# The expert loop's tiles in another sequence, a fourth raw buffer, and second products that take all high parts first

## Chip, cores and metric

One core of a Trainium2 chip. The metric is the device time of one execution in microseconds (us), and lower is better. TensorE's clock has two levels, 1.2 and 2.4 GHz, and the profile gives the granted level as a share of the higher one.

## What is computed

Three parts follow each other. The first is attention over 4 x 8 heads of 576 positions (one attention on means of four positions, one in a narrow window). The second is a mixture of experts, and the change touches only this one. The third is a token and channel mixing network. The reference of the second part, cut to what matters:

```python
for s in range(S):
    e = fresh_e if s == 0 or local_gate[b, s] < 0.5 else prev_e
    h = np.maximum(x[b, s] @ w1[e], 0.0)      # 512 -> 1024
    out[b, s] = p[e] * (h @ w2[e])            # 1024 -> 512
```

## The kernel before

**Number format.** Every float32 operand of the expert products is split into a high and a low part (both of a type that TensorE multiplies at its full rate), and a product is made of three matmuls: high times high, high times low, low times high (`three`, L1125). So each weight block costs a cast on ACT (`wh`) and a subtraction on DVE (`wl`), and each hidden block costs a ReLU on ACT (`hh`) and one operation on DVE (`hl`, `relu`, L1132).

**The expert loop** (`Moe.run`, L1477) goes over eight ranks of experts, most tokens first, with room for 384, 376, 320, 288, 256, 256, 192 and 128 tokens (`CAPS`), and for each over eight blocks of 128 hidden columns. A block loads 512 KB of raw weights into a `raw` tile (`fetch`, L1196, on SP's queue), splits them (`loadw`, L1205), makes the first product into a PSUM tile `m` (`mm1`, L1236), and one block later the second product into one to three PSUM tiles `y` of 128 tokens each (`mm2`, L1269). There are two `m` and four `y` tiles. After an expert's last block the `y` tiles are copied to `yo` and stored to `yd`. The tokens of an expert are fetched by indirect transfers from POOL into `xg` (`gather`, L1215), 128 at a time, transposed by TensorE and split into `xh` and `xl`. Five `xg` tiles exist, three `raw` tiles, and a ring of four `wh` and four `wl` (one of each, `l_wh` and `l_wl`, is filled before the loop). For the last expert (128 tokens) the first product reads `raw` and `xg` directly. In between, 21 jobs convert the weights of the mixing stage (`convert`, L1141: `cr`, `cf`, `cs`, on DVE, ACT and POOL), and a memset on POOL and ten stores on SP zero the unused rows of `yd` (`zeros`, L1464).

**The order of the work** comes from a planner in the kernel (`Sched.order`, L406). It keeps for every engine the time at which it is free, takes the operation that can start first (ties within 0.02 go to the longer remaining path less a stage time), and hands each operation a free tile of its pool. The engines then execute the lists in order. All matmuls of an `mm2` are one operation for it. It plans each stage by itself, from time 0. For the expert loop TensorE counts as free from 2.0 (`PE_LATE`) and all others from 0.

**Where tiles lie.** A tile lies behind the one allocated before it. The loop's tiles take over bytes of attention's tiles, and the first writer of a tile waits for the last users of the bytes below. In bytes of a partition, attention's tiles are: pt0 and pt1 141760 to 154048, kd 154048 to 158656, vd 158656 to 166848, od and ptd to 176064, p0 and p1 176064 to 180160, pc0 180160 to 182208, pc1 to 184256, xn to 188352, small ones above. p and pc hold results of two experts that are computed early, and are stored to `yd` by transfers from ACT's queue; pc's are the last work before the loop. The loop's tiles of before are: cr, cf, cs, yo and h 105376 to 137120, zero to 139168, raw0 to raw2 139232 to 151520, wh0 to wh2 to 163808, wl0 to wl2 to 176096, xg0 176096 to 178144, xg1 to 180192, xg2 to 182240, xg3 to 184288, xg4 to 186336, xh0 and xl0 to 198624.

Of the kernel before, what the change touches and what calls it, by code (L numbers as in the profile page):

```python
# [4 lines left out]
F32 = mybir.dt.float32  # L5
F32R = mybir.dt.float32r
BF16 = mybir.dt.bfloat16
F16 = mybir.dt.float16
I32 = mybir.dt.int32
# [8 lines left out]
DM = H * D  # L18
# [6 lines left out]
CAPS = [384, 376, 320, 288, 256, 256, 192, 128]  # L25
# [10 lines left out]
KF = FF // 128  # L36
# [1138 lines left out]
class Experts:  # L1175
# [11 lines left out]
    after = first = ready = ()  # L1187
# [78 lines left out]
    def hidden(self, C):  # L1266
        return self.new("hh")[:, 0:C], self.new("hl")[:, 0:C], None

    def mm2(self, r, fb, h):  # L1269
        S_ = self.S  # L1270
        hh, hl, both = h
        C = self.caps[r]
        T = -(-C // 128)
        wh, wl = (w[:, DM:2 * DM] for w in self.w[KF * r + fb][0:2])
        m = 0 if both is None else self.part(C)
        if fb == 0:
            self.y = [self.new("y") for _ in range(T)]
        for k in range(T):
            if k % self.CUT == 0:
                g = S_.group("pe", after=self.after)  # L1280
                g.__enter__()
            n = min(128, C - 128 * k)
            c = slice(128 * k, 128 * k + n)
            if n == m:
                two = [(2 * n, both, wh), (n, hh[:, c], wl)]
                for rows, x, w in two if fb == 0 else two[::-1]:
                    S_.i("pe", "matmul", out=self.y[k][0:rows], lhsT=x, rhs=w, start=(fb == 0 and rows > n), stop=(fb == KF - 1 and rows > n))
            else:
                three(S_, self.y[k][0:n], (hh[:, c], hl[:, m + c.start:m + c.stop]), (wh, wl), fb == 0, fb == KF - 1)
            if (k + 1) % self.CUT == 0 or k == T - 1:  # L1290
                g.__exit__(None, None, None)
        if self.ready:
            self.after = self.first + (len(S_.ops) - 1,)
        if fb == KF - 1:
            for k in range(T):
                n = min(128, C - 128 * k)
                t = self.result(r, k)
                if n == m:
                    self.i("act", "copy", out=t[0:n], in_=self.y[k][n:2 * n])
                    self.i("dve", "tensor_tensor", out=t[0:n], in0=t[0:n], in1=self.y[k][0:n], op=ALU.add)  # L1300
                elif k % 2 == 0:
                    self.i("act", "copy", out=t[0:n], in_=self.y[k][0:n])
                else:
                    self.i("dve", "tensor_copy", out=t[0:n], in_=self.y[k][0:n])
                r0 = self.rows[r] + 128 * k
                self.i(self.QUEUE, "dma_start", out=self.yd[r0:r0 + n, :], in_=t[0:n])
# [115 lines left out]
class Moe(Experts):  # L1422
    LO, CUT, QUEUE = "dve", 4, "dma"

    def __init__(self, ctx, tc, at, rt, xd, yd, wx, jobs, lead):
        self.rt, self.xd, self.jobs = rt, xd, jobs
        S_ = Sched(tc)
        pool = lambda n, b, **kw: ctx.enter_context(tc.tile_pool(name=n, bufs=b, reuse_waits="tile", **kw))
        sa, sp, pt, pp = pool("ma", 1), pool("ms", 1), pool("mt", 1, space=PSUM), pool("mp", 1, space=PSUM)
        self.sp = sa  # L1430
        for name, shape, dt, n in (
            ("cr", [128, 1024], I32, 2), ("cf", [128, 512], I32, 2), ("cs", [128, 512], F32, 2),
            ("yo", [128, DM], F32, 3), ("h", [128, 2 * CAPS[0]], F32R, 3),
            ("raw", [128, 1024], F32, RAW), ("wh", [128, 1024], F32R, RING - NLEAD), ("wl", [128, 1024], F32R, RING - NLEAD),
            ("xg", [128, DM], F32, 5), ("xh", [128, 4, CAPS[0]], F32R, 1), ("xl", [128, 4, CAPS[0]], F32R, 1),
        ):
            p = sp if name in ("raw", "wh", "wl", "xg", "xh", "xl") else sa
            S_.pool(name, [p.tile(shape, dt, name=f"{name}{j}") for j in range(n)])
        for name, n in (("t", 2), ("m", 2), ("y", 4)):
            S_.pool(name, [(pt if name == "t" else pp).tile([128, 512], F32, name=f"{name}{j}") for j in range(n)])  # L1440
        super().__init__(S_, tc, at, yd, wx, CAPS, ROW0, lambda r: rt.eri[0:1, r:r + 1],
                         lambda r, k, n: rt.xi[0:n, r, k:k + 1], xd[:, :])
        self.ident = at.ident
        self.held = {n: [S_.held(n, t) for t in ts] for n, ts in lead.tiles.items()}
        self.x[0] = tuple(self.held[n][0] for n in ("xh", "xl"))
        for n in range(NLEAD):
            self.w[n] = self.held["wh"][n], self.held["wl"][n], None
# [29 lines left out]
    def run(self):  # L1477
        NW = KF * NE
        prev, done = None, []
        t0 = 0.0  # L1480
        for n in range(NW):
            r, fb = divmod(n, KF)
            self.S.stage = t0
            t0 += 4 * (12 * CAPS[r] / 2400 + TILES[r] * 0.65)
            if n >= NLEAD:
                self.loadw(n)
            if fb == 3 and r + 1 < NE:
                self.gather(r + 1)
            h = self.mm1(r, fb)
            if prev is not None:  # L1490
                self.mm2(*prev)
            prev = (r, fb, h)
            done.append(len(self.S.ops) - 1)
            if n == 24:
                self.S.stage = t0
                self.zeros()
            if n >= 8 and n % CONV == 0 and self.jobs:
                self.S.stage = t0 + 60
                convert(self.S, *self.jobs.pop(0), after=(done[n - 6],))
        self.mm2(*prev)  # L1500
        assert not self.jobs
        self.S.issue(self.S.order(busy=dict(pe=PE_LATE)))
        at, cold = self.at, self.S.pools["t"][1][0][:, 264:512]
        for _ in range(TAIL):
            self.nc.tensor.matmul(cold, at.onesb, at.rb, start=True, stop=True)
# [270 lines left out]
KDVE = ((0, 0), (0, 1), (1, 0), (1, 1), (2, 0), (2, 1), (3, 0), (3, 1))  # L1776
STEP, D_LEAD, R_LAG = 14.0, 2.0, 0.5
SLACK = 0.02
PE_LATE = 2.0
NLEAD, CONV, C2_EARLY = 1, 2, 4  # L1780
RAW, RING = 3, 4
RING_F, TOK_FB = 26, 3
MIX_WARM = 10.0, 0.5
MARK = 1, 0
SHIFT = {('d1', 0): -6, ('load_q', 0): -11, ('x1', 3): 14, ('load_u', 0): 1, ('route', 2): -8, ('load_u', 3): -14, ('d1', 1): 14, ('route', 3): 18, ('x1', 0): 5, ('l1', 3): 2, ('l1', 0): -5, ('d2', 2): -1, ('Lead', 'gather'): -8, ('Early', 'gather'): -22, ('l2', 3): 2, ('pool_k', 1): -2, ('l2', 1): 1, ('pool_v', 3): -4, ('route', 1): 3, ('Early', 'mm2'): 2, ('pool_q', 0): -4, ('d1', 3): 3, ('pool_q', 2): -10, ('pool_k', 0): -5, ('load_q', 3): 1, ('pool_q', 3): -1, ('load_u', 1): 1, ('load_u', 2): 7, ('l2', 2): -2, ('d2', 0): -5, ('load_q', 2): 3}
WARM0 = 0.0
# [23 lines left out]
```

## Time and profile before

| | us |
|---|---|
| median of 3 runs | 817.35 |
| lowest and highest | 811.60 and 822.07 |
| the profiled execution, its time | 818.32 |
| the profiled execution, its span | 816.5 |
| mean granted TensorE clock | 0.982 |

The span has three stages: attention up to about 205 us, the expert loop up to 441.9 us, and after a hand-over of some ten the mixing stage to the end. The profile is of one execution. Its rows give, for every instruction, its engine, the line of the kernel, the tiles that it writes and reads, its start and duration, and in brackets the idle time before it with what ended that. All loop instructions are issued from lines L548 to L552, so the tiles' names tell them apart: `m` is a first product, `y` a second one, `t` a transpose. An arrow `<-` reads "made from" between tiles and "released by" before an engine.

### The profile page before, as it was taken

What the parts mean: (1) busy time and instruction counts of PE and PEld (TensorE: products, weight loads), DVE (VectorE), ACT (ScalarE), POOL (GpSimd) and SP (SyncE); (2) the same over time, 40 slices, a digit from 0 to 9 for tenths busy, and PEclk for the clock granted to TensorE, in tenths of its full rate; (3) what the DMA queues carried; (4) which work ended last, traced back from release to release, by engine and by line L of the source; (5) the groups of instructions that cost most, each with busy time, mean ns of one, the idle gap of its engine ahead of it and who ended that gap; (6) DMA issues with size and microseconds to landing.
All of it is one profiled execution on the core that took longest, in us unless ns stands there. A gap on an engine that the chain in (4) does not pass through costs nothing. (4 is left out here: it accounts for less than half of the span.)

```text
span 816.5 us, 14043 instructions
## 1 busy us (share of the span) xinstructions
PE 768.3 (94%) x5377; PEld 645.6 (79%) x5377; DVE 468.9 (57%) x1064; ACT 331.3 (41%) x722; POOL 195.9 (24%) x158
## 2 busy tenths in 40 slices
PE   7878898999899998999898999999999999999998
PEld 5666775898787977887796787888888888888897
DVE  6789898698366878889952667532441244121121
ACT  1767886554344554666552535320321032111110
POOL 3325313111423545525400155200000000000000
PEclk9999999999899999999999999999999999999999
DMA  9988344556588775867653224002000200010010
GB/s 267 223 224 225 98 130 129 165 176 238 187 295 287 248 255 170 279 224 253 205 196 133 82 91 123 26 26 71 14 1 26 71 14 1 0 52 1 1 52 27
DMA packets 36348, 107.92 MB, mean 132 GB/s; under 512 B 5003, under 2 KB 5643, under 8 KB 35895
## 3 DMA queue, kind: packets, MB, share of 16 engines
q1 hardware_dynamic: 32359, 95.15, 37.1%
q0 software_dynamic: 3200, 10.28, 4.2%
q10 hardware_dynamic: 720, 1.57, 0.5%
q8 instruction: 43, 0.70, 0.4%
q14 instruction: 26, 0.21, 0.1%
HBM read 87.32 MB, written 19.66 MB: 131 GB/s over the span
## 5 line engine op out<-in xcount | busy, mean ns | idle before, releaser
L552 DVE SCALAR_TENSOR_TENSOR x_h<-x_m,x_h 128x512 fp32r<-128x512 f32 (+1 forms) x60 | 38.2, 637 | 194.9 <-ACT x_h L552 192.5
L548 PE MATMUL x_y<-x_h,c2h 128*128 128x512 f32 (+1 forms) x480 | 136.2, 369 | 0.0
L552 ACT ACTIVATE x_h<-x_m 128x512 fp32r<-128x512 f32 (+1 forms) x60 | 33.3, 555 | 201.0 <-PE x_m L548 176.0
L548 PEld LDWEIGHTS x_y<-x_h,c2h 128*128 128x128 f32 x480 | 86.6, 189 | 14.4
L548 PE MATMUL x_y<-x_h,c2l 128*128 128x512 f32 (+1 forms) x240 | 88.3, 368 | 0.0
L548 PE MATMUL y<-wh,h 128*128 128x512 f32 (+2 forms) x205 | 75.9, 408 | 4.2 <-DVE h L552 2.8
L552 DVE TENSOR_TENSOR wl<-raw,wh 128x1024 fp32r<-128x1024 f32 (+1 forms) x47 | 60.4, 1287 | 19.7 <-ACT wh L552 19.2
L552 ACT CAST wh<-raw 128x1024 fp32r<-128x1024 f32 (+1 forms) x47 | 46.9, 1001 | 25.6 <-PE y L548 15.5
L552 POOL TENSOR_SCALAR cs<-cs 128x512 f32<-128x512 f32 (+1 forms) x21 | 38.0, 1810 | 57.6 <-ACT cs L552 57.2
L548 PEld LDWEIGHTS x_y<-x_h,c2l 128*128 128x128 f32 x240 | 45.2, 189 | 7.6
L548 PEld LDWEIGHTS y<-wh,h 128*128 128x128 f32 (+2 forms) x205 | 38.7, 190 | 15.4 <-DVE h L552 5.0
L548 PE MATMUL y<-wl,h 128*128 128x512 f32 (+3 forms) x112 | 44.7, 399 | 0.0
L552 POOL TENSOR_TENSOR cf<-cf,cs 128x512 f32<-128x512 f32 (+1 forms) x21 | 37.7, 1797 | 28.2 <-DVE cf L552 26.4
L552 DVE SCALAR_TENSOR_TENSOR h<-m,h 128x256 fp32r<-128x256 f32 (+3 forms) x88 | 29.4, 356 | 10.1 <-ACT h L552 9.9
L1169 POOL DMA_INDIRECT xg<-xd,q_xi x19 | 19.4, 1020 | 56.2 <-PE t L550 19.5
L552 ACT ACTIVATE h<-m 128x256 fp32r<-128x256 f32 (+6 forms) x64 | 25.4, 397 | 17.7 <-PE m L548 14.6
L552 DVE SCALAR_TENSOR_TENSOR cf<-cr,cf 128x512 int32<-128x512 int32 (+1 forms) x42 | 30.4, 725 | 0.7
L548 PE MATMUL m<-l_xh,wh 128*128 128x256 f32 (+2 forms) x96 | 29.2, 304 | 1.0 <-DVE h L552 1.0
L548 PE MATMUL y<-l_wh,h 128*128 128x512 f32 (+2 forms) x75 | 28.8, 424 | 1.3 <-DVE h L552 1.1
L548 PE MATMUL pv<-pt,vw 128*64 128x96 f32 x384 | 22.5, 263 | 7.6 <-ACT pt L552 4.6
L548 PE MATMUL m<-l_xh,wl 128*128 128x256 f32 (+2 forms) x96 | 28.8, 300 | 0.0
L548 PE MATMUL m<-l_xl,wh 128*128 128x256 f32 (+2 forms) x96 | 28.8, 300 | 0.0
(813 smaller groups left out, 2022.0 us busy)
## 6 DMA issues: line engine op xcount, KB each, us to landing
raw<-in_wx SPq DMA_DIRECT2D x80, 512.0 KB
cr<-in_c SPq DMA_DIRECT2D x16, 512.0 KB
vw<-in_vw SPq DMA_DIRECT2D x12, 512.0 KB
kz<-in_kw SPq DMA_DIRECT2D x24, 200.0 KB
xd<-xn SPq DMA_DIRECT2D x16, 256.0 KB
yd<-zero SPq DMA_DIRECT2D x8, 512.0 KB
yd<-yo SPq DMA_DIRECT2D x15, 256.0 KB
x_cr<-in_c SPq DMA_DIRECT2D x7, 512.0 KB
```

What stands on the lines that cost most here:

```text
L548: f(kw.pop("out"), **kw)
L552: f(**kw)
L1169: nc.gpsimd.indirect_dma_start(out=t.real()[0:n, :], out_offset=None, in_=table, in_offset=bass.IndirectOffsetOnAxis(ap=index, axis=0))
```

## The change

The tiles of the loop are allocated in the sequence of two lists of names (`PLACE`). The first list has the same sequence as before. The second one puts the xg tiles behind the raw tiles, and ends with wl1. There are four raw tiles. The planner counts TensorE as free from 8.0, ACT from 6.5 and DVE from 7.5. In `mm2` of the loop (not of the two experts computed early, whose `CUT` is 1) a new function `halves` issues, for all tiles, high times high and high times low, and after them low times high for all tiles. The number of matmuls stays.

By the sizes of the tiles the second list gives: raw0 to raw3 139232 to 155616, xg0 to xg4 155616 to 165856, xh0 to 172000, wh0 to 176096, wh1 to 180192, wh2 to 184288, wl2 to 188384, wl0 to 192480, xl0 to 198624, wl1 to 202720.

```diff
+    def halves(self, fb, h, ys, wh, wl, m):
+        hh, hl, both = h
+        mm = lambda y, x, w, start, stop: self.S.i("pe", "matmul", out=y, lhsT=x, rhs=w, start=start, stop=stop)
+        first, last = fb == 0, fb == KF - 1
+        o = 0
+        two = []
+        for k, y in enumerate(ys):
+            n = y.a.shape[0]
+            c = slice(o, o + n)
+            o += n
+            if n != m:
+                mm(y, hh[:, c], wh, first, False)
+                mm(y, hh[:, c], wl, False, False)
+                two.append((y, hl[:, m + c.start:m + c.stop], wh, False, last))
+            else:
+                tall = self.y[k][0:2 * n]
+                if first:
+                    two += [(tall, both, wh, True, False), (y, hh[:, c], wl, False, False)]
+                else:
+                    mm(y, hh[:, c], wl, False, False)
+                    two.append((tall, both, wh, False, last))
+        for x in two:
+            mm(*x)
...
-        for k in range(T):
+        if self.CUT >= T:
+            with S_.group("pe", after=self.after):
+                self.halves(fb, h, [self.y[k][0:min(128, C - 128 * k)] for k in range(T)], wh, wl, m)
+        for k in range(T) if self.CUT < T else ():
...
-        self.S.issue(self.S.order(busy=dict(pe=PE_LATE)))
+        self.S.issue(self.S.order(busy=LATE))
...
-PE_LATE = 2.0
+LATE = dict(pe=8.0, act=6.5, dve=7.5)
...
-RAW, RING = 3, 4
+RAW, RING = 4, 4
...
+PLACE = ("cr0 cr1 cf0 cf1 cs0 cs1 yo0 yo1 yo2 h0 h1 h2",
+         "raw0 raw1 raw2 raw3 xg0 xg1 xg2 xg3 xg4 xh0 wh0 wh1 wh2 wl2 wl0 xl0 wl1")
```

## Rows read from the trace of the kernel before

**Rows 1.** The page's first part: busy us, share of the span, instructions of each engine.

```profile
PE 768.3 (94%) x5377; PEld 645.6 (79%) x5377; DVE 468.9 (57%) x1064; ACT 331.3 (41%) x722; POOL 195.9 (24%) x158
```

**Rows 2.** Table by stretches: length, busy us by engine, clock, transfer share, GB/s.

```profile
204.85:217.66 12.81, 8.95 (x39) 7.68 (x37) 4.71 (x6) 4.35 (x7) 7.24 (x8) 0.73 0.44 138
217.66:322.80 105.14, 99.42 (x524) 86.79 (x522) 74.46 (x110) 51.19 (x81) 45.95 (x29) 1.00 0.77 256
322.80:327.65 4.85, 4.83 (x18) 4.10 (x19) 3.17 (x6) 3.08 (x6) 1.11 (x1) 0.65 0.64 188
...
340.00:400.00 60.00, 55.63 (x343) 47.31 (x342) 55.64 (x76) 36.40 (x59) 29.47 (x17) 1.00 0.71 234
...
424.30:434.70 10.40, 8.64 (x58) 7.39 (x56) 4.03 (x9) 4.10 (x11) 0.00 (x0) 1.00 0.72 225
434.70:440.40 5.70, 5.68 (x31) 5.15 (x31) 1.97 (x4) 2.13 (x5) 0.00 (x0) 0.70 0.29 119
```

**Rows 3.** List of TensorE's waits, 204 to 442: us in total, times, longest.

```profile
PE y L548 <- DVE h L552: 3.9, 6, 1.0
PE t L550 <- DMA xg<-xd,q_xi: 3.9, 1, 3.9
PE m L548 <- DVE h L552: 2.9, 3, 1.5
PE m L548 <- DMA raw<-in_wx: 1.8, 1, 1.8
PE m L548 <- DVE wl L552: 1.8, 1, 1.8
PE y L548 <- DVE yo L552: 1.3, 3, 0.6
```

**Rows 4.** The loop's start, by engine: start, duration, engine, operation, idle before.

```profile
205.08 0.34 PE L548 MATMUL m<-l_xh,l_wh 128*128 128x384 f32 x1
207.18 0.60 PE L550 MATMUL t<-ident,xg 128*128 128x128 f32 x4
...
217.69 0.42 PE L548 MATMUL m<-l_xh,wh 128*128 128x384 f32 x1
...
208.19 0.94 POOL L1169 DMA_INDIRECT xg<-xd,q_xi  x1 [16.41 <-DMA yd<-pc]
...
194.95 1.45 SPq L1200 DMA_DIRECT2D raw<-in_wx  x3
...
205.31 0.93 ACTq L552 DMA_DIRECT2D yd<-pc  x2
207.37 0.49 ACT L552 ACTIVATE h<-m 128x384 fp32r<-128x384 f32 x1 [1.50 <-PE m L548]
...
212.76 0.59 ACT L552 CAST xh<-t 128x512 fp32r<-128x512 f32 x1 [4.36 <-PE t L550]
213.24 1.99 ACT L552 CAST wh<-raw 128x1024 fp32r<-128x1024 f32 x2
...
214.32 2.36 DVE L552 TENSOR_TENSOR wl<-raw,wh 128x1024 fp32r<-128x1024 f32 x2 [0.25 <-issue]
```

**Rows 5.** List of waits of SP's queue, 204 to 442.

```profile
SPq L552 <- POOL zero L546: 20.5, 1, 20.5
```

**Rows 6.** In order of time: TensorE's four transposes and the next product.

```profile
329.93 0.60 PE L550 MATMUL t<-ident,xg 128*128 128x128 f32 x4
330.29 0.38 PE L548 MATMUL m<-xh,l_wh 128*128 128x288 f32 x1
```

**Rows 7.** In order of time: a second product's wait for DVE's h.

```profile
379.06 0.40 PE L548 MATMUL y<-wh,h 128*128 128x512 f32 x1
379.30 0.39 PE L548 MATMUL y<-wl,h 128*128 128x512 f32 x1
380.65 0.73 PE L548 MATMUL y<-wh,h 128*128 128x512 f32 x2 [0.96 <-DVE h L552]
```

More of the change, by code (lines that the diff above doesn't have):

```diff
@@ L1430, in __init__ @@
         self.sp = sa
[L1431 to L1438, printed above, removed]
+        shapes = dict(cr=([128, 1024], I32), cf=([128, 512], I32), cs=([128, 512], F32), yo=([128, DM], F32),
+                      h=([128, 2 * CAPS[0]], F32R), raw=([128, 1024], F32), wh=([128, 1024], F32R), wl=([128, 1024], F32R),
+                      xg=([128, DM], F32), xh=([128, 4, CAPS[0]], F32R), xl=([128, 4, CAPS[0]], F32R))
+        tiles = {}
+        for p, names in ((sa, PLACE[0]), (sp, PLACE[1])):
+            for x in names.split():
+                name, j = x.rstrip("0123456789"), x[len(x.rstrip("0123456789")):]
+                tiles.setdefault(name, {})[int(j)] = p.tile(*shapes[name], name=x)
+        for name, ts in tiles.items():
+            S_.pool(name, [ts[j] for j in sorted(ts)])
         for name, n in (("t", 2), ("m", 2), ("y", 4)):
```

## The prediction

> **What bounds the kernel now.** I read the page first, for the shares: TensorE is busy for 94% of the span and no other engine for more than 57% [rows 1]. So only time that TensorE lacks can be gained, and the question is where it lacks any. The change touches one stage, the expert loop, which runs from about 205 to 441.9 us. I took the table by stretches next [rows 2], then the list of TensorE's waits inside that loop [rows 3]. In it the reader sees eight kinds of wait, and the six largest add up to 3.9 + 3.9 + 2.9 + 1.8 + 1.8 + 1.3 = 15.6 us. To these come three stretches at a granted clock below 1: 0.73, 0.65 and 0.70 [rows 2]. Each of them begins with one of the long waits (3.9, 1.8 and 1.8 us). In the last two the lower of the two levels (1.2 instead of 2.4 GHz) costs 4.85 x 0.35 = 1.7 us and 5.7 x 0.30 = 1.7 us on top of the wait. The mixing stage behind the loop is TensorE alone and none of its instructions change.
>
> Then I read the loop's first 13 us in order of time [rows 4]. TensorE does the first product of block 0 from 205.08 to 207.18, a group of four transposes, and stops. The transposes of the next rows wait for a gather that POOL could only issue at 208.19, released by the transfer yd<-pc. The ACT queue then shows the consequence: the cast xh at 212.76 comes after 4.36 us of idle time, and the cast of block 1's weights, wh, stands behind it at 213.24, although the raw weights were asked for at 194.95. Block 1's first product starts at 217.69.
>
> Why a gather waits for a transfer out of pc can be seen in the addresses. The gather's target xg1 covers bytes 178144 to 180192, and pc0 begins at 180160: they share 32 bytes. xg2 and xg3 lie on pc0 and pc1 wholly.
>
> The same transfer also stops SP. The memset of the zero tile is in POOL's queue behind those gathers, and SP waited 20.5 us for it [rows 5]. Every later raw load is behind that in SP's queue.
>
> **The change, part by part.** The sum is made against the profiled execution: 818.32 us, of which 816.5 are the span and 1.8 lie around it. That is 0.97 above the median of the runs shown.
>
> *Sequence of tiles and the planner's start times, taken together.* After the change the five xg tiles lie at 155616 to 165856, on kd and vd, which attention has left long before. So POOL can issue five gathers without the wait for yd<-pc, the memset follows them, and SP is no longer held. The planner now believes that TensorE comes free at 8.0, ACT at 6.5 and DVE at 7.5 instead of at 2, 0 and 0. With raw weights landing before that, I expect its list to put the casts of blocks 1 to 3 first on ACT, then h of block 0, and on TensorE block 0's first product, block 1's first product, block 0's second product. The transposes then move to where their stage time puts them, about block 3.
>
> What the old start costs: from 205.08 to 217.69 are 12.6 us. The work in it at full clock is 2.1 for the product (twelve, to 207.18), four groups of transposes at 0.36 (329.93 to 330.29 [rows 6]), so 1.4, and nine products of 512 columns at 0.23 to 0.24 (379.06 to 379.30 [rows 7]), so 2.1: 5.6 us. The excess is 7.0 us.
>
> What the new start costs: ACT is done with its last transfer of attention at 205.31 + 0.93 = 206.24. A cast takes 1.0 and DVE's wl 1.18 [rows 4], so wl of block 1 is there at 208.4. The first two products of block 1 need only wh; the third stops TensorE from about 207.2 to 208.4: 1.2 us. The wait for pc doesn't vanish either. It moves to the weights: wh1 now covers 176096 to 180192, again 32 bytes of pc0, and wh2 lies on pc0 and pc1. ACT's second cast so starts at about 208.2, the third ends at 210.2, and h of block 0 (0.49) behind them at 210.7, against block 1's first product ending at 208.4 + 10 x 0.17 = 210.1 (2.1 over twelve is 0.17): 0.6 us. Queued behind those casts on ACT are h and, through h, DVE's lower half. Sum: 7.0 - 1.8 = 5.2 us gained. Bounds: 7.0 if the list hides both stalls, and 1.5 if the new gap of 1.2 grows to the 1.8 that let the clock fall elsewhere (0.6 + 1.7) and the casts cost another 1.4 behind pc. I take 5.2, because every term of it has a row.
>
> *High parts first.* No product is added or removed, and no weight load. What moves is the place of the first product that needs DVE's half of h. TensorE waited 3.9 us in six places for it [rows 3], all between 369 and 402 us, where blocks have 256 columns and two tiles. One of the six is shown [rows 7]: two products at 379.06 and 379.30, then 0.96 us idle. The old order already put two products ahead of the wait; the new one puts four. So the cover grows by 2 x 0.23 = 0.46 us, not by the whole wait. Six waits so give 6 x 0.46 = 2.8 us at most. DVE is busy for 55.64 of the 60 us there [rows 2], so a part of what is gained will be late again at the next subtraction for wl. Ends: 0 and 2.8; I take 2.0.
>
> The same move has a price at the seven changes of expert. There the second and third tile's accumulators are asked for 0.23 and 0.46 us sooner, while yo still empties them. Three such waits are in the list, 1.3 us together [rows 3]. Ends: 0 and 3 x 0.46 = 1.4; I take +0.7.
>
> *Fourth raw buffer.* It adds no transfer. Its cover is for the last expert, whose blocks of 128 columns are so short that weights come late: one wait of 1.8 us [rows 3], then 1.7 us through the clock [rows 2], 3.5 in all. A fourth load in flight can remove both if the transfer engines have room. They moved 225 GB/s at a share of 0.72 there, against 256 GB/s at 0.77 as a mean over the loop's first 105 us [rows 2], so there is some room. Ends: 0 and 3.5; I take 2.5. The Trainium skill ("Trainium Kernel Development and Optimization", Key Constraints) speaks against it: transfers from SP, ACT and POOL all run on the same 16 engines, so another load in flight makes none faster. If those engines were the limit in the tail, this term would be 0 and the time 809.8; the row of 0.72 says that they aren't.
>
> *The middle.* The list is planned anew from other start times, so the remaining waits (m for DVE's h 2.9, wl 1.8 with 1.7 of clock [rows 2, 3]) will fall elsewhere. They come from DVE being late against its plan, which the change doesn't mend. A load that is there sooner lets ACT's casts go sooner, and DVE has 30.7 us to spare from 217.66 to 322.80 [rows 2]. Ends: -6.4, all gone, and +3.5, one more stall like the one at 322.8 (wait and clock). I take -1.0.
>
> Sum: -5.2 - 2.0 + 0.7 - 2.5 - 1.0 = -10.0 us. 818.32 - 10.0 = 808.3, and 0.97 lower against the median: 807.35. I predict 807.
>
> **The rivals.** *Everything goes.* The start gives 7.0, high parts 2.8, the tail 3.5 and the middle half or all of its 6.4: together 16.5 to 19.7, so 797 to 801. For it speaks DVE's spare time early in the loop; against it 93% busy DVE at 340 to 400.
>
> *Little of it stays.* Either the waits are kept per pool and not by bytes, so that the gather goes on waiting and only other terms gain, or what the terms behind the start win is lost again at DVE in 340 to 400. Then 1.5 to 5.2 remain, and the time is 812 to 816. Against the first: the loop's first three raw loads were issued at 194.95, ten us before pc's transfer [rows 4], so waits don't go by pools. DVE's 93% speaks for the second.
>
> *The tail stays.* If the transfer engines and not the buffers set the pace of the last expert, a fourth load in flight lands no sooner and the 2.5 is missing: 809.8. For it speaks that 225 GB/s is the highest that its stretch shows; against it the 256 GB/s that the loop's first half holds for 105 us. The Trainium skill's rule above would have it so.
>
> *Slower.* At a change of expert the new order wants all accumulators at once while yo stands in DVE's queue behind a wl of 1.2 us. The largest such wait is 0.6 [rows 3]. If it grows to 1.8, the clock falls as at 322.8, and one change of expert costs 1.2 + 1.7 = 2.9. Four of the seven (11.6) give back the 10.7 that the rest brings; all seven would add 20.3, less 10.7: 827. So 818 to 827. Against it: 0.46 more than 0.6 is 1.1, below each of the waits after which the clock fell.
>
> **How the numbers follow.** Forecast (802 to 811): 0.50. The tail stays (809.8): 0.12. Everything goes (797 to 801): 0.14. Little stays (812 to 816): 0.17. Slower (818 to 827): 0.07. A measurement of this kernel can tell about 2% from no change, that is 16.3 us: below 801 is faster, above 833.7 slower. Faster so gets the 0.14 and a little of the forecast's lower edge, 0.15; slower 0.01 for a mishap beyond the last rival's end; same 0.84. For eight in ten I take the forecast and the tail's case, most of "little stays" up to 815 and the near half of "everything goes", down to 799. The forecast's own range is 802 to 811.
>
> **What the profile after would show.** The start is right if no gather waits for yd<-pc, SP no longer waits for zero, and block 1's first product begins within 5 us of block 0's; wrong if TensorE still idles over 2 us there or the clock falls. The move of the wait is right if a cast of wh now waits for yd<-pc. High parts first is right if TensorE's waits for DVE's h sum to under 2 us. The tail is right if no wait for raw is left after the last expert begins. The prediction fails if the middle holds new stalls over 1.7 us with the clock down behind them, or if the mixing stage, taken as unchanged, changes.

## The result and the profile after

| | before | after |
|---|---|---|
| median, us | 817.30 (20 runs, 809.23 to 822.07) | 810.04 (20 runs, 805.98 to 814.77) |
| ratio | | 0.9916, 95% interval 0.9895 to 0.9937 |
| the profiled execution: time and span, us | 818.32 and 816.5 | 806.79 and 804.9 |
| mean granted clock | 0.982 | 0.993 |

The changed kernel is 7.3 us faster (5.1 to 8.6 by the interval), which is under 2%. 807 was predicted, with a range from 799 to 815.

The first part of the page after answers to [rows 1]. TensorE lost 8.1 us of busy time, although it executes the same 5377 matmuls. In the table by stretches below, 5.8 of them lie in the three stretches (B, D and E) whose mean clock was under 1 before: products at the lower clock take longer, and fewer are executed at it.

```profile
PE 760.2 (94%) x5377; PEld 640.5 (80%) x5377; DVE 466.6 (58%) x1064; ACT 331.4 (41%) x722; POOL 196.8 (24%) x158
```

To see where the time went, I cut both traces at the same five instructions: POOL's first gather of the early experts' rows, TensorE's first product of the loop, the first product of the second expert, that of the fourth, that of the last (which reads `raw`), and the end of the last second product. This gives five stretches, called A to E from here on. Table by stretches of the kernel before (columns as in [rows 2]):

```profile
182.08:205.08 23.00, 22.45 (x139) 19.37 (x138) 19.97 (x76) 9.68 (x16) 3.97 (x4) 1.00 0.67 229
205.08:240.66 35.58, 31.72 (x155) 28.64 (x154) 17.05 (x21) 13.78 (x19) 12.53 (x11) 0.90 0.73 236
240.66:313.60 72.94, 68.98 (x363) 59.39 (x362) 54.17 (x82) 39.01 (x63) 36.00 (x23) 1.00 0.77 256
313.60:424.27 110.67, 103.69 (x624) 88.73 (x624) 93.70 (x143) 62.23 (x100) 43.17 (x25) 0.98 0.68 229
424.27:442.07 17.80, 16.02 (x96) 13.74 (x95) 6.89 (x15) 6.68 (x16) 0.00 (x0) 0.90 0.51 169
```

The same of the kernel after:

```profile
182.11:208.76 26.65, 22.70 (x139) 19.36 (x138) 20.15 (x76) 9.78 (x16) 8.42 (x9) 1.00 0.83 274
208.76:238.38 29.62, 28.88 (x151) 25.92 (x150) 19.07 (x25) 15.41 (x22) 8.02 (x6) 1.00 0.84 294
238.38:306.58 68.20, 67.81 (x368) 60.33 (x366) 51.91 (x79) 37.99 (x60) 33.03 (x23) 1.00 0.73 247
306.58:415.38 108.80, 101.91 (x623) 87.57 (x624) 91.77 (x143) 61.57 (x101) 46.33 (x26) 1.00 0.70 233
415.38:430.59 15.21, 14.88 (x96) 12.28 (x95) 6.88 (x15) 6.69 (x16) 0.00 (x0) 1.00 0.52 164
```

A is the stretch just ahead of the loop, and it became 3.65 us longer. B is the first expert, C the second and third, D the next four, E the last. B lost 6.0, C 4.7, D 1.9 and E 2.6 us. The mixing stage with the hand-over, taken as unchanged, is 374.5 us before and 374.3 after.

TensorE's waits inside the loop after the change, as in [rows 3]:

```profile
PE m L548 <- DVE wl L552: 2.4, 2, 1.8
PE y L548 <- DVE h L552: 2.3, 4, 0.8
...
PE m L548 <- DVE h L552: 1.1, 1, 1.1
PE y L548 <- DVE yo L552: 0.8, 1, 0.8
...
PE m L548 <- DMA raw<-in_wx: 0.2, 1, 0.2
```

The wait for a gather is gone, that for raw is down to 0.2 us, and the one long wait for wl stands as it was. The loop's start in order of time, which answers to [rows 4] and [rows 5]:

```profile
208.76 0.34 PE L548 MATMUL m<-l_xh,l_wh 128*128 128x384 f32 x1
...
209.00 0.92 ACTq L552 DMA_DIRECT2D yd<-pc  x2
...
210.02 3.15 ACT L552 CAST wh<-raw 128x1024 fp32r<-128x1024 f32 x3 [0.47 <-ACT pc L552]
...
211.10 3.51 DVE L552 TENSOR_TENSOR wl<-raw,wh 128x1024 fp32r<-128x1024 f32 x3 [2.13 <-ACT wh L552]
211.12 0.44 PE L548 MATMUL m<-l_xh,wh 128*128 128x384 f32 x1
...
212.38 0.44 PE L548 MATMUL m<-l_xh,wl 128*128 128x384 f32 x1 [0.64 <-DVE wl L552]
...
214.22 0.39 PE L548 MATMUL y<-l_wh,h 128*128 128x512 f32 x1
```

Block 1's first product now begins 2.36 us behind block 0's (12.61 before), and block 0's second product follows it at 214.22. Only one wait of 0.64 us stands between them. The transposes come in a later block.

### The profile page after: what moved, and what is told of

It reads as the page before. It is cut to its first block, busy times and chain, and to the rows that moved or that the text cites. A ratio compares the mean times of both kernels' runs of the same rounds, so it can differ in the third digit from the quotient of the medians.

```text
span 804.9 us, 14042 instructions
## 1 busy us (share of the span) xinstructions
PE 760.2 (94%) x5377; PEld 640.5 (80%) x5377; DVE 466.6 (58%) x1064; ACT 331.4 (41%) x722; POOL 196.8 (24%) x158
## 5 line engine op out<-in xcount | busy, mean ns | idle before, releaser
L548 PE MATMUL y<-wh,h 128*128 128x512 f32 (+2 forms) x205 | 71.9, 401 | 2.7 <-DVE h L552 1.5
L552 DVE TENSOR_TENSOR wl<-raw,wh 128x1024 fp32r<-128x1024 f32 (+1 forms) x47 | 58.6, 1250 | 18.5 <-ACT wh L552 16.3
L548 PE MATMUL y<-wl,h 128*128 128x512 f32 (+3 forms) x112 | 41.4, 393 | 0.0
L548 PEld LDWEIGHTS pv<-pt,vw 128*64 128x64 f32 x384 | 17.4, 141 | 13.3 <-ACT pt L552 5.3
```

Of the source, the lines that this page charges most:

```text
L548: f(kw.pop("out"), **kw)
L552: f(**kw)
```

## The experiments

Traces with the same code ahead of the loop and behind it can differ by some 4 us in these stages: A begins at 182.1 in the first trace of the changed kernel and at 186.0 in the second, and what lies behind E takes 374.3 to 379.1 us over the fourteen traces. So each experiment is read in two ways: its timed ratio to the kernel before, and the stretches A to E of its trace, cut at the same instructions.

| kernel | ratio (95%) | A | B | C | D | E | sum |
|---|---|---|---|---|---|---|---|
| before | | 23.00 | 35.58 | 72.94 | 110.67 | 17.80 | 260.0 |
| before, second trace (b_again) | 0.9995 (0.9964 to 1.0027) | 23.33 | 35.37 | 72.49 | 110.15 | 16.25 | 257.6 |
| + second products (b_halves) | 1.0015 (0.9981 to 1.0049) | 23.64 | 35.25 | 74.80 | 110.78 | 15.85 | 260.3 |
| + fourth raw (b_raw4) | 0.9870 (0.9816 to 0.9925) | 22.81 | 34.95 | 72.79 | 107.21 | 15.41 | 253.2 |
| + sequence (b_place) | 0.9907 (0.9872 to 0.9941) | 25.09 | 28.89 | 71.90 | 110.99 | 16.00 | 252.9 |
| + start times (b_late) | 0.9972 (0.9936 to 1.0008) | 22.69 | 37.94 | 67.65 | 109.51 | 15.47 | 253.3 |
| after | 0.9916 (0.9895 to 0.9937) | 26.65 | 29.62 | 68.20 | 108.80 | 15.21 | 248.5 |
| after, second trace (a_again) | 0.9877 (0.9835 to 0.9920) | 27.31 | 29.64 | 69.13 | 109.80 | 15.11 | 251.0 |
| - second products (a_no_halves) | 0.9921 (0.9894 to 0.9947) | 27.15 | 30.43 | 69.26 | 109.03 | 14.81 | 250.7 |
| - fourth raw (a_raw3) | 0.9932 (0.9905 to 0.9960) | 27.18 | 29.62 | 67.78 | 109.52 | 16.08 | 250.2 |
| - sequence (a_old_place) | 0.9965 (0.9927 to 1.0003) | 23.64 | 37.15 | 69.77 | 110.05 | 14.00 | 254.6 |
| after, planner's order only (a_gate) | 0.9905 (0.9869 to 0.9941) | 25.72 | 29.57 | 67.68 | 109.22 | 15.33 | 247.5 |
| after, gathers held back (a_gate2) | 0.9884 (0.9842 to 0.9926) | 24.33 | 31.18 | 68.26 | 109.08 | 15.06 | 247.9 |
| after, gathers spread (a_spread) | 0.9881 (0.9832 to 0.9930) | 23.70 | 29.62 | 69.42 | 109.90 | 14.84 | 247.5 |

By the two pairs of traces (b_again and a_again), one kernel repeats within 0.7 us in A, 0.2 in B, 0.9 in C, 1.0 in D and 1.6 in E. A sum repeats within 2.5 us.

**The changed kernel once more.** No edit.

> The changed kernel once more, unaltered, for its time and a second trace. Theory: the loop's five gathers, issued by POOL right behind the early experts' three, share the 16 transfer engines with the early experts' raw loads and so hold up the work ahead of the loop; then this trace shows again a first product of the loop at about 208.8 us (205.1 before), with TensorE idle for 3 to 4 us between 187 and 196. Rival: that stall was chance in one execution; then the first product lies at about 205 and the time is 3 to 4 us below the first profile's 806.8. Ratio to the kernel before: 0.990 to 0.993 by the first, 0.987 by the second.

A was 27.31 us, with the same two stalls (2.9 and 1.1 us), so they weren't chance. That is read from the trace alone: the ratio of 0.9877 lies nearer to the rival's 0.987, and its interval holds the expectation's 0.990 too. The profiled execution took 814.36, 7.6 us more than the first trace's: 3.9 of them lie ahead of A, 2.5 in A to E and 1.2 behind.

**The kernel before once more.** No edit.

> The kernel before, unaltered, for a second trace of it. What is compared between kernels from here on is the stretch from the early experts' first gather to the loop's first product (23.0 us in the first trace) and the loop (first product to the end of the last second product, 237.0 us), because the stages ahead of and behind these differ by up to 4 us between traces of kernels that have the same code there. Expected: 22.8 to 23.7 and 236.5 to 237.5. If the loop lies more than 1 us away from 237, differences of 1 us between kernels can't be read from single traces.

A and B repeated. The loop was 234.3 us and not 237.0, so differences of 1 us can't be read from single traces' loops. More than half of the difference lies in E, where the clock did not fall this time. Table by stretches of this trace, E:

```profile
424.58:440.83 16.25, 14.61 (x96) 12.43 (x95) 6.98 (x15) 6.68 (x16) 0.00 (x0) 1.00 0.55 186
```

The wait for raw was there, with 1.6 us against 1.8 [rows 3], but no lower clock followed it.

**The stalls ahead of the loop.** In the changed kernel POOL issues the loop's five gathers right behind the early experts' three, 1.28 us apart. POOL in order of time, after:

```profile
184.80 0.94 POOL L1169 DMA_INDIRECT xg<-xd,q_xi  x1 [0.30 <-issue]
186.05 0.99 POOL L1169 DMA_INDIRECT xg<-xd,q_xi  x1 [0.30 <-issue]
...
191.18 0.95 POOL L1169 DMA_INDIRECT xg<-xd,q_xi  x1 [0.30 <-issue]
192.13 0.54 POOL L546 MEMSET zero<- 128x512 f32 x1
```

TensorE and ACT in the same stretch, after:

```profile
191.15 0.51 PE L548 MATMUL sl<-kz2x,pd0x 128*128 128x512 f32 x1 [2.81 <-ACT pd0x L552]
194.99 0.50 PE L548 MATMUL sl<-kz3x,pd2x 128*128 128x512 f32 x1 [1.11 <-ACT pd2x L552]
```

```profile
190.72 0.38 ACT L552 ACTIVATE pd0x<-g 128x256 fp32r<-128x256 f32 x1 [4.46 <-remote]
```

ACT stops first; TensorE and DVE (3.05 us) then wait for its pd0x. Before, the same ACT instruction ran at 186.96, at once behind its product:

```profile
186.96 0.38 ACT L552 ACTIVATE pd0x<-g 128x256 fp32r<-128x256 f32 x1 [0.55 <-PE g L548]
```

A first experiment told the planner that the gathers may come only behind block 0:

```diff
             if fb == 3 and r + 1 < NE:
+                self.first = (done[0],)
                 self.gather(r + 1)
+                self.first = ()
```

> The changed kernel with one thing altered: every gather of the loop may only start when block 0's hidden block is done, so none runs beside the early experts' loads (the memset of the zero tile thereby stands ahead of them in POOL's list). Nothing else of the order moves. Theory (gathers hold up the early experts' raw loads): the loop's first product is back at about 205, and the time is about 3.5 us below the changed kernel's, ratio to before 0.987; the transposes of the next expert come only about 12 us later in TensorE's list, so they don't wait. Rival 1 (the 3.7 us later start has another cause, such as a wait that the planner's later start times or the new bytes put there): first product stays at about 208.8, time unchanged. Rival 2: the early gathers were needed; TensorE waits at the transposes and the time is above the changed kernel's.

This was a miss of construction: such an `after` orders the planner's list, and no engine waits for it. POOL issued the five from 187.00 to 193.14, one of them 2.04 us long, with the memset ahead. TensorE's two stalls came to 2.5 us, A to 25.72, and the question stayed open. The second one makes POOL wait in truth (`behind` is block 0's hidden block, set for the first gather alone; shown in part, the rest sets these names and puts the memset of zero behind block 0 in the planner's order):

```diff
+            if self.behind is not None:
+                b = self.behind[:, 0:16].bitcast(F32)
+                S_.i("pool", "tensor_tensor", after=self.first, out=t[:, 0:16], in0=b, in1=b, op=ALU.mult)
+                self.behind = None
             gather(S_, t, n, self.table, self.index(r, k, n), self.first)
...
```

> The changed kernel with a true wait ahead of the loop's gathers: POOL first multiplies 16 columns of block 0's hidden block into the first gather's tile, so none of the five gathers (nor the memset of zero behind them) can be issued before about 208 us. In the altered kernel of the run before (a_gate) only the planner's order said so, and POOL issued them as early as in the changed kernel. Theory: issuing five more gathers behind the early experts' three stops TensorE, ACT and DVE together for 2.8 us near 188 and for 1.1 us near 195; here both stalls are gone (at most the 0.5 us that the kernel before shows), the stretch from the early experts' first gather to the loop's first product is 3.5 us shorter than in the changed kernel (23.0 us in the kernel before, 26.7 in the changed one), and the loop itself loses less than 1.5 us, because the transposes come only after block 3. Time about 807 where the changed kernel has 809 to 810. Rival 1: the stall doesn't come from the gathers; the stretch stays at 26.7. Rival 2: the stall goes along with the gathers and appears right behind them, at 208 to 215, inside the loop; then the time doesn't change.

POOL issued the five from 213.21 on. The stall at pd0x is gone. One of 1.9 us for pd2x is left, where the kernel before has 0.5 us and its second trace 0.9. A fell from 26.65 and 27.31 to 24.33. B rose by 1.6, a little more than the 1.5 that the theory allowed the whole loop, which took 223.6 us here beside 221.8 and 223.7 in the changed kernel. So in the changed kernel the stall at pd0x comes with the early gathers. The third one leaves the gathers early and only spreads them (`fill` is 3 for ranks 1 to 3, else 0):

```diff
-def gather(S_, t, n, table, index, after=()):
+def gather(S_, t, n, table, index, after=(), fill=0):
...
     def f():
+        for _ in range(fill):
+            nc.gpsimd.memset(t.real(), 0.0)
```

> The changed kernel with three memsets of the gather's own tile ahead of each gather of ranks 1 to 3 on POOL (the gathers write over them, the output stays the same), so the five early gathers are issued some 3 us apart instead of 1.28 us; TensorE's, ACT's and DVE's lists are those of the changed kernel. Theory A (the transfers themselves crowd out the early experts' raw loads and what releases them, when they come packed): the stalls of 2.8 and 1.1 us near 188 and 195 shrink to less than 2 us together. Theory B (the bytes have to be moved before the loop either way, packed or not): the waits move, but the stretch from the first gather to the first product stays at 26.5 to 27.3 us. In the kernel with a true wait ahead of the gathers it was 24.3.

POOL in this kernel's order of time, TensorE's longest wait, and its table by stretches, A:

```profile
188.17 0.95 POOL L1171 DMA_INDIRECT xg<-xd,q_xi  x1 [0.27 <-POOL xg L1170]
189.12 1.71 POOL L1170 MEMSET xg<- 128x512 f32 x3
191.10 0.95 POOL L1171 DMA_INDIRECT xg<-xd,q_xi  x1 [0.27 <-POOL xg L1170]
```

```profile
192.49 0.50 PE L548 MATMUL sl<-kz3x,pd2x 128*128 128x512 f32 x1 [1.26 <-ACT pd2x L552]
```

```profile
182.55:206.25 23.70, 22.41 (x139) 19.29 (x138) 20.36 (x76) 9.79 (x16) 17.97 (x24) 1.00 0.89 309
```

With 2.9 to 4.5 us between them, the same five gathers cost nothing that a trace can tell: A is 23.70, where the traces without early gathers have 22.69 to 23.64. By its numbers theory A holds against theory B. Its mechanism, raw loads that are crowded out, is not what stopped ACT: pd0x reads no raw weights, and during ACT's stop the queues had nearly the shares of the transfer engines that they had in the kernel before, though SP's moved 0.73 instead of 0.88 MB. Shares by queue from 186.3 to 190.7 (q1 is SP's, q0 POOL's; packets, MB, share), after and before:

```profile
q1 hardware_dynamic: 193, 0.73, 48.1%
q0 software_dynamic: 168, 0.56, 33.1%
```

```profile
q1 hardware_dynamic: 240, 0.88, 49.5%
q0 software_dynamic: 172, 0.56, 32.4%
```

Over the whole of A the engines moved more in a_spread than in any other kernel (309 GB/s at a share of 0.89), so their room was not what ran out in the changed kernel (274 at 0.83). The Trainium skill ("DMA: Bandwidth & Descriptors", Queues, rings and completion order) states that each engine takes turns between the queues' packets; by that, packed gathers would slow the raw loads beside them, but ACT's 4.46 us don't end with a load in the trace, so no run here shows that it is the cause.

The row's "remote" says only that no instruction ended where ACT was released. The semaphore events in the traces say a little more. ACT waited for the semaphore that TensorE raises behind pd0x's product g. In eight of the fourteen traces it rises 0.01 to 0.02 us behind the product's end, in the two of the changed kernel and in those of a_no_halves and a_raw3 3.75 to 3.86 us behind it, and in a_gate 1.74. In the fourteenth, b_place (below), POOL issues the same gathers just as tightly up to that point, and the semaphore rises in time. There ACT's casts wait 2.70 and 2.04 us for raw loads instead (0.98 and none before), and A is 25.09. So no trace has the late semaphore without these gathers issued early and 1.3 us apart, but one has the gathers without it. a_spread also brings the gathers later (the last at 201.59 instead of 191.18), so it doesn't part spacing from lateness. What held the semaphore is not shown, and this stays open.

a_spread is also the fastest form by the stretches, with a_gate: 247.5 beside 248.5 and 251.0 of the changed kernel, which is within the repeat of a sum. Its time (808.06 median) can't be told from the changed kernel's 809.0 in a_again, so the cost of the early gathers is seen in traces and in no timed ratio.

**One part of the change alone, on the kernel before.** The sequence, with three raw tiles in use (raw3's bytes stay empty), the old start times and second products (shown in part):

```diff
+PLACE = ("cr0 cr1 cf0 cf1 cs0 cs1 yo0 yo1 yo2 h0 h1 h2",
+         "raw0 raw1 raw2 raw3 xg0 xg1 xg2 xg3 xg4 xh0 wh0 wh1 wh2 wl2 wl0 xl0 wl1")
...
```

> The kernel before with the new sequence of tiles alone: three raw tiles in use (the fourth one's bytes left empty), the planner's old start times, the old order of second products. Theory: no gather waits for yd<-pc and SP not for zero, so the loop's first block loses its 3.9 us wait for a gather and the clock stays up, but the five gathers run together with the early experts' loads, so the stretch from the early experts' first gather to the loop's first product is 26.7 us instead of 23.0. The first product to the second product's end: 12.6 + 2 us before, 8 to 10 here, since TensorE still does the transposes first and ACT their casts. Net 0 to 3 us below the kernel before. Rival: the sequence alone brings all of the start's gain; 5 us or more below.

The rival came closer. B fell by 6.6 us, all of what it falls in the changed kernel, and the ratio is 0.9907. Block 1's first product begins 5.9 us behind block 0's, with no idle time: the transposes run there, and their gathers are there already. So the new sequence gains as much with the transposes first as the changed kernel does with them later. (Its trace is of an execution of 818.16 us, beside a median of 810.66; A and B are read from it alone.) Table by stretches of this kernel, B:

```profile
210.95:239.84 28.89, 28.89 (x155) 26.39 (x154) 16.73 (x21) 13.73 (x19) 9.58 (x7) 1.00 0.77 258
```

The start times alone:

```diff
-PE_LATE = 2.0
+LATE = dict(pe=8.0, act=6.5, dve=7.5)
```

> The kernel before with the planner's three later start times alone: old sequence, three raw tiles, old second products. Theory: the start's gain comes from the list rather than from where the tiles lie: with TensorE counted as free from 8, ACT from 6.5 and DVE from 7.5 the planner puts the transposes, which wait for the late gather, behind block 1's first product and block 0's second, so the 3.9 us wait and the lower clock go although the gather is as late as before. The loop is 8 to 10 us shorter than 237, with no early-gather stall ahead of it (23 us to the first product); 808 to 810. Rival: the gathers behind yd<-pc hold the memset of zero and through it SP's raw loads, so blocks 3 and 4 wait for raw or wh, and the loop is within 4 us of 237.

The theory failed for B and the rival's mechanism is there: SP waits behind zero, behind the gathers, behind yd<-pc. SP's waits, ACT and TensorE in order of time, and the stretches B and C of this kernel:

```profile
SPq L552 <- POOL zero L546: 18.1, 1, 18.1
```

```profile
224.61 1.04 ACT L552 CAST l_wh<-raw 128x1024 fp32r<-128x1024 f32 x1 [11.13 <-DMA raw<-in_wx]
```

```profile
226.10 0.79 PE L548 MATMUL y<-wh,h 128*128 128x512 f32 x1 [3.43 <-ACT h L552]
```

```profile
207.36:245.30 37.94, 32.98 (x151) 27.25 (x150) 17.00 (x24) 14.58 (x22) 13.81 (x11) 0.91 0.82 279
245.30:312.95 67.65, 67.65 (x367) 60.25 (x366) 52.48 (x80) 37.74 (x59) 34.30 (x23) 1.00 0.70 244
```

The first raw load behind zero is issued only after 217, ACT is idle for 11.13 us, and h, queued on ACT behind that cast, stops TensorE for 3.43 us; the clock is 0.91. But C, where the kernel before leaves TensorE idle for 3.96 us (72.94 less 68.98), has no idle time at all. So the start times bring nothing at the start without the sequence, and 5 us in the second and third expert, which was not forecast. The time shows less than the stretches: 0.9972 is 2.3 us, and its interval holds 1.

The new second products alone, `halves` on the kernel before:

```diff
+        if self.CUT >= T:
+            with S_.group("pe", after=self.after):
+                self.halves(fb, h, [self.y[k][0:min(128, C - 128 * k)] for k in range(T)], wh, wl, m)
...
```

> The kernel before with the new order inside a second product alone. Theory: TensorE's waits for DVE's h at second products fall from 3.9 us to 2.0 to 2.6, those for yo rise by up to 0.7; 1 to 2 us below the kernel before, all of it between 340 and 402 us. Rival: the waits move to wl or m; no difference.

No gain (1.0015). TensorE's waits of this kernel, from 175 to 445:

```profile
PE m L548 <- DVE h L552: 5.3, 4, 2.0
...
PE y L548 <- DVE h L552: 3.5, 7, 0.8
```

The waits of y for DVE's h fell by only 0.4 us from the first trace of the kernel before (3.9) and not at all from the second (3.5), and those of m for DVE's h rose from 2.9 [rows 3] and 2.5 (second trace) to 5.3. The rival had it: what is not waited for at one product is waited for at another. That DVE delivers no sooner would explain it, and is argued here and not shown.

The fourth raw tile alone, which shifts all later tiles by 4096 bytes:

```diff
-RAW, RING = 3, 4
+RAW, RING = 4, 4
```

> The kernel before with a fourth raw tile alone, in the old sequence, so all tiles behind raw lie 4096 bytes higher. Theory: the wait for raw in the last expert (1.8 us) and the lower clock behind it (1.7) go: 3.5 us less in the last 20 us of the loop. At the start all five xg tiles now lie on pc or above it, so the first gather waits for pc too, and the start costs up to 1.3 us more (one more gather behind yd<-pc). Net 2 to 3.5 us below. Rival: the transfer engines set the pace of the last expert; a wait for raw above 1 us stays there.

The tail is as expected: the wait for raw is 0.4 us and E 15.41. The start doesn't get worse by more than its scatter, although its wait for gathers is 5.4 us in two places. That D is 3 us shorter here was not expected. It does not come back in the changed kernel, which has the same D with three raw tiles (109.52) as with four (108.80 and 109.80), and was not followed further. The ratio (0.9870, from four runs) is more than the 5.6 us of the stretches explain.

**One part undone, in the changed kernel.** The old sequence:

```diff
-         "raw0 raw1 raw2 raw3 xg0 xg1 xg2 xg3 xg4 xh0 wh0 wh1 wh2 wl2 wl0 xl0 wl1")
+         "raw0 raw1 raw2 raw3 wh0 wh1 wh2 wl0 wl1 wl2 xg0 xg1 xg2 xg3 xg4 xh0 xl0")
```

> The changed kernel with the old sequence (and so with xg on pc again), but with its four raw tiles, its start times and its second products. Theory (the list makes the gain, the sequence only moves the gathers): no stall of 2.8 and 1.1 us near 188 and 195, the first product 23 to 24 us behind the first gather, the loop 222 to 225; the time is 2 to 4 us below the changed kernel's, 806 to 808. Rival (the prediction's reading: the wait for yd<-pc must be taken from the gathers and from SP): the loop's start has 3 us or more of waits for a gather or for raw again, loop 227 or more, time 812 or more.

Both halves of the theory were met in A (23.64, no early stall), and it failed in B, where the rival held. SP's waits and ACT in order of time of this kernel:

```profile
SPq L552 <- POOL zero L546: 20.1, 1, 20.1
```

```profile
220.73 1.04 ACT L552 CAST wh<-raw 128x1024 fp32r<-128x1024 f32 x1 [7.41 <-DMA raw<-in_wx]
```

TensorE then waits 3.8 us for DVE's xl, queued behind the cast. B is 7.5 us longer than in the changed kernel, A 3.3 shorter, and of the gain over the kernel before less than half is left in the time: 0.9965. The sequence alone is worth what the prediction gave to sequence and start times together, and it acts through SP and the raw loads as much as through the gather.

The old second products, with the planner's lists unchanged:

```diff
-        if self.CUT >= T:
+        if False:
...
-        for k in range(T) if self.CUT < T else ():
+        for k in range(T):
```

> The changed kernel with the old order inside a second product (each tile's three products together); the planner's lists stay as they are, so only the place of the wait for DVE's half of h differs. Theory: TensorE's waits for DVE's h at second products are 1.5 to 2.5 us more than the 2.3 of the changed kernel and its waits for yo a few tenths less; time 1 to 2 us above the changed kernel's, ratio to it 1.0012 to 1.0025. Rival: halves gives nothing, since what is not waited for at h is waited for at the next wl; ratio 1.000.

TensorE's waits for DVE's h at second products were 3.3 us in five places against 2.3 and 2.4 in four, and for yo 0.6 against 0.8. So the new order takes away 1.0 us, where 1.5 to 2.5 was expected, and gives back 0.2. The sum of the stretches (250.7) and the ratio (0.9921) don't differ from the changed kernel's beyond their scatter, so the rival (no gain in the time) is not refuted.

Three raw tiles, the fourth one's bytes left empty:

```diff
-            S_.pool(name, [ts[j] for j in sorted(ts)])
+            S_.pool(name, [ts[j] for j in sorted(ts)][:RAW if name == "raw" else None])
...
-RAW, RING = 4, 4
+RAW, RING = 3, 4
```

> The changed kernel with three raw tiles in use; the fourth one's bytes stay empty, so all other tiles lie as in the changed kernel. Theory: the wait for raw in the last expert comes back (1.8 us) and with it the lower clock behind it (another 1.7); 2.5 to 3.5 us above the changed kernel's time, all behind 420 us. Rival: the wait went because the plan, not the number of buffers, moved; then no wait for raw above 0.5 us and the time within 1 us of the changed kernel's.

The wait for raw came back with 1.4 us and E is 0.9 us longer, at a clock of 1.00. The lower clock did not come back, so by the trace the lost time is that of the wait alone, and the 2.5 to 3.5 us of the expectation were too many. The time doesn't decide it: 0.9932 is 0.0016 above the changed kernel's first ratio and 0.0055 (4.5 us) above that of a_again.

## Why the prediction was right, and which of its steps were not

Point by point, against the mean of the two traces of either kernel (A 23.2 to 27.0, B 35.5 to 29.6, C 72.7 to 68.7, D 110.4 to 109.3, E 17.0 to 15.2; sum 258.8 to 249.7):

| step | predicted | shown |
|---|---|---|
| loop's start (B) | -5.2 | -5.85 |
| gathers issued early (A) | 0, no term | +3.8 |
| high parts first | -2.0 + 0.7 for yo | -0.8 in the waits, under the scatter in the time |
| middle (C and D) without high parts | -1.0 | about -4.4: -5.2 for C and D less the 0.8 above |
| tail (E) | -2.5 | -1.9 |
| sum | -10.0 | -9.1 by stretches, -7.3 by the medians |

**Loop's start.** The mechanism through the addresses was right in each link: no gather waits for yd<-pc, SP no longer waits for zero, and block 1's first product begins 2.36 us behind block 0's. a_old_place and b_late showed the reverse: with xg on pc, zero holds SP for 18 to 20 us and B is 37 to 38 us. The other half of the mechanism, the planner's list that puts block 1's product ahead of the transposes, brings nothing here: b_place has the old list and a B of 28.89, beside 29.62 with the new one. Of the two new stalls (1.2 and 0.6 us) only the first appeared, with 0.64. By the forecast's own rows it should have been 0.8, as the two products that need only wh take 0.35 of the 1.2. The check "a cast of wh now waits for yd<-pc" came true, but the wait was 0.10 us instead of about 1: the first of the three casts ends at 211.07 and the second starts at 211.17, released by that transfer. ACT in order of time, the second trace (0.15 us):

```profile
215.73 1.05 ACT L552 CAST wh<-raw 128x1024 fp32r<-128x1024 f32 x1 [0.15 <-DMA yd<-pc]
```

The forecast had let that transfer end 2.9 us behind its issue (205.31 to 208.19 [rows 4]); here it was issued from 209.00 on and released the cast 2.2 us later.

**Early gathers: the step that was left out.** "POOL can issue five gathers without the wait" was costed as a pure gain. No sentence said what the gathers run beside once they come sooner (four of the five by 21 us, the first by 5), and that was the early experts' work with its raw loads. The move cost 3.8 us, as much as the tail and the high parts together were to bring. a_gate2 and a_spread show that the gathers are needed for it: with them held back, or 2.9 us and more apart, A is 24.33 and 23.70. b_place shows that they are not the whole cause of the long stall, and how they stop ACT stays open. The prediction did ask whether the 16 shared transfer engines have room, but only in the tail, where their share is 0.52 and the wait for raw went away. By the Trainium skill's rule ("Trainium Kernel Development and Optimization", Key Constraints) that all these queues share the same 16 engines, the place to look was where the transfers are moved to; the bytes alone don't explain the stall, as a_spread's 0.89 and the nearly equal shares during the stall show.

**The middle.** The sum escaped the missing 3.8 us because this term was too small by as much: -4.4 instead of -1.0, inside the bounds of -6.4 to +3.5. The sentence that failed is that the waits "come from DVE being late against its plan, which the change doesn't mend". b_late shows that the start times do mend a part: C is 67.65 with them and 72 to 75 without (b_raw4 72.79, b_halves 74.80). In the changed kernel TensorE's idle time in C fell from 3.96 to 0.39 us, and DVE's work there from 54.17 to 51.91. What did stay is the one long wait for wl, 1.75 us at 315.78 in place of 1.78 at 322.8. Its clock cost went all the same (below), but that isn't shown to be what D gained: in a_no_halves the clock fell there again, and its D (109.03) is as short as the changed kernel's.

**High parts first.** The cover did grow, but 2.0 of an upper end of 2.8 us was too much: 1.0 us came by a_no_halves, at most 0.4 by b_halves, and none that a time shows. The caution that what is won "will be late again" at DVE was right, and b_halves shows where: at m, for DVE's h. The check "under 2 us" failed with 2.3, and with 3.4 if the waits of m for DVE's h are counted. The price at yo did not come as a sum: 0.8 us in one wait, against 1.3 in three.

**Tail.** The wait for raw fell from 1.78 to 0.2 us, so "the tail stays" is refuted; a_raw3 brings it back. The conclusion that another load in flight makes none faster does not hold in this tail. The term was too large because it counted the lower clock behind the wait as sure, and b_again had the wait without it.

**Rivals.** "Everything goes" would have needed 7.0 at the start and all of the tail. "Little of it stays" is refuted in its first condition, as waits go by bytes; its second, the loss at DVE, holds for high parts alone. "Slower" is refuted: waits for yo fell.

So the total was right, and by its own steps the prediction got the start (through the addresses, not through the list) and the tail, missed a loss of 3.8 us and undersized a gain by 3.4. These two cancelled, which is luck.

## What to carry to other kernels

When a wait is taken from a transfer, ask what it will run beside at its new time: a gather that need not be there early can be held back or spread out, which made A 2.3 to 3.6 us shorter in the traces here, though no time showed it. A wait taken off one engine's queue should be followed through every queue behind it; here gather, memset, store and raw load made one chain, and cutting it at its head (where the tiles lie) was worth more at the loop's start than planning around it. A planner's start times move its whole list, so their effect has to be sought through the stage and not only at its start.

## What the runs showed that was not expected

A wait of the same length was followed by the lower clock in some traces and not in others. Before, the wait for wl of 1.78 us at 322.82 was followed by a granted clock of 0.66 over the next 5 us, and by the same in the second trace (1.79 us, 0.66). Table by stretches, before:

```profile
322.66:327.65 4.99, 4.83 (x18) 4.10 (x19) 3.31 (x7) 3.08 (x6) 1.25 (x1) 0.66 0.62 182
```

After the change, behind 1.75 us at the same product, the clock stayed at 2.4 GHz, and so it did in the second trace (1.77 us):

```profile
315.70:320.70 5.00, 4.87 (x27) 3.79 (x28) 3.32 (x7) 3.74 (x6) 1.68 (x2) 1.00 0.62 185
```

18 matmuls were executed in the one stretch, 27 in the other. It is no property of the kernel's sequence, list or second products alone. Thirteen of the fourteen traces have this wait with 1.75 to 1.79 us, and the clock fell behind it in three: both of the kernel before, and a_no_halves, which is the changed kernel but for the second products. Table by stretches, a_no_halves (1.77 us):

```profile
320.88:325.88 5.00, 4.92 (x19) 3.79 (x20) 3.33 (x7) 3.30 (x6) 1.16 (x1) 0.66 0.65 185
```

All three have the old second products, but b_late has them too, and its clock stayed up, as in the other nine. What TensorE did ahead of the wait doesn't part them either: some nine us earlier it had waited 1.46, 1.25 and 1.01 us where the clock fell, and where it stayed from nothing (b_late) to 1.42 us (b_halves). In the tail, 1.78 us were followed by a mean of 0.90 over E, and 1.59, 1.4 and 1.2 us by 1.00. A forecast should give the clock's price behind a wait of such a length as an end of the range and not as a sure term.
